# Pooled attention and a rotated channel mixer on one core: another way to load the queries of batch 1, twelve matmuls ahead of the rest, the last stores split over two queues, and a new order of pieces

## The chip, the core and the metric

One NeuronCore of a Trainium2 chip runs the whole kernel. The metric is the device time of one execution in microseconds, as the median of repeated executions. Engines in what follows: PE multiplies matrices and turns tiles (its weight loads are listed as PEld), DVE, ACT and POOL work on elements, SP only issues DMAs.

## What is computed

The attention has 8 batches of 8 heads with 576 positions of 64 channels; its keys and values are first averaged over groups of 8 positions, so that each query meets 72 keys. Its output, put side by side into 512 channels, goes through a layer that rotates by learned angles, mixes over positions and channels, and adds a gated copy.

```python
k_p = k.reshape(B, H, S // 8, 8, D).mean(axis=3); v_p = v.reshape(B, H, S // 8, 8, D).mean(axis=3)
attn = softmax(q @ k_p.T / sqrt(D)); x = (attn @ v_p) put to [B, S, H * D]
theta = x @ w_theta
y = w_tok_r @ (x * cos(theta)) + w_tok_i @ (x * sin(theta))      # over positions
u = x + y
out = u + maximum(u @ w_ch, 0)
```

All four weight matrices arrive as 64-bit floats and are read as pairs of 32-bit words; everything else is 32-bit.

## The kernel before

The work is cut into pieces, each a Python generator whose steps issue a few instructions. For batch b there are: `k`/`K` and `v`/`V` (load keys and values by parts, and add up groups of 8; for batch 0 PE adds them with an identity, L509, for the others POOL or DVE, L435 and L440), `Q` (load queries and turn them so that channels lie on partitions), `S` (scores of 128 positions on PE, L662, the maximum on DVE, L693, the exponential on ACT, L702 or L713, then the division, L727 and L734), `E` or the last steps of `S` (turn the probabilities), `X` (probabilities times values, L856, which gives x by channels in the tile xT), `T` (angles on PE, L879, sine and cosine on ACT, x turned back on PE, L889, and the products z on DVE, L906 and L908), `Z` (split z into a rounded part zh and a rest zl, L930), `M` (the mix over positions, L944, and u = x + y, L950), and `F` (the channel product, L973, the gate, L979, a 32x32 turn, L992, and four stores by SP, L998). A product of two 32-bit matrices is made of three products of rounded parts.

Before the first mix the weights have to be made: `h` (w_theta), `w` (the two position matrices, part 0 and 1 of five row blocks), `W` (their turning on PE, L389 and L392, and the split into WTh on ACT or DVE and WTl on DVE, L400) and `c` (w_ch). The 64-bit floats are put together in `to_f32` (L284 to L317): a scaling on ACT (L292), the low word (L296 on ACT, L298 on DVE or POOL), a sign (L303 on ACT, L305 on DVE or POOL), two integer steps on DVE (L307, L309) and a product (L316 on DVE or POOL).

What order things have is written out by hand in a table, `SCHEDULE` (L30): each word names a piece and issues its next step, and a letter at its end (v, g, a) sets which of DVE, POOL and ACT does the step where there is a choice. Every engine, and SP's queue of DMAs, runs its own instructions in the order of the table and stops at the first one whose input or buffer is not ready.

For batch 0 the queries are loaded by rows, 128 positions of all heads at a time, and turned on PE (`queries_on_pe`, L550, five pieces, with a copy from PSUM by ACT or DVE, L572). For all other batches they are loaded in 16 DMAs of 72 KB, already cut into 32x32 blocks, and DVE turns the blocks (`queries`, L535, two pieces, L547).

```python
EARLY, EXACT, V_ON_PE, K_ON_PE, Q_ON_PE, SUMS_ON_ACT = 2, 1, 1, 1, 1, 2   # L136
for word in SCHEDULE.split():                                              # L1079
    name, engine = (word[:-1], word[-1]) if word[-1] in "vga" else (word, None)
    now[0] = engine
    next(streams[name])
```

## Time and profile before

| what | us |
| --- | --- |
| executions of the kernel: median of 3 (lowest, highest) | 629.72 (628.58, 631.18) |
| the profiled execution, own time | 627.23 |
| its span on the core | 625.5 |
| scores of batch 0's first tile start on PE | 20.23 |
| first mix product (L944) starts on PE | 84.36 |
| first channel product (L973) starts on PE | 121.29 |
| last matmul ends | 619.87 |

The span runs from the first to the last instruction of the profiled execution, which is one of many and here 0.4% under the median of the others. Busy time counts from the start of an instruction to its end, so an instruction that has begun and is held up inside still counts as busy. A stretch of the span tells more than the whole, since the opening (weights and batch 0), the middle and the end have different limits.

### The profile page before, as it was taken

The page shows a single profiled execution, that of the slowest core. Times are in us where ns is not written, and L with a number is a line of the kernel's source. Part 1 is how long each engine was busy: PE and PEld are TensorE (multiplying, and loading weights), DVE is VectorE, ACT ScalarE, POOL GpSimd, SP SyncE. Part 2 cuts the span into 40 slices and gives each one's busy share as a digit, 9 for nine tenths or more (in the row PEclk, how much of TensorE's full clock was granted, in tenths as well). Part 3 has the DMA queues.
Part 4 walks back from the last instruction along what each step waited for, and adds up shares of the span by engine and source line. Part 5 has one row for each costly group of instructions (what it writes and reads, how often), then busy time and mean ns, then how long its engine had stood idle before and what let it go on. Part 6 is the DMA issues. An engine that isn't in the chain of part 4 may idle for free.

```text
span 625.5 us, 11352 instructions
## 1 busy us (share of the span) xinstructions
PE 586.4 (94%) x4076; PEld 541.6 (87%) x4076; DVE 490.0 (78%) x898; ACT 306.4 (49%) x658; POOL 338.4 (54%) x371
## 2 busy tenths in 40 slices
PE   4899889999789999999999999999999989999996
PEld 3765789978689989998999999988999989989996
DVE  5679988888898889898868687798967798856324
ACT  4798858678822564228622762236335443044010
POOL 4566445766766677466463668547445652622230
PEclk9999989999999999999999999999999999999998
DMA  9896202376454555655357346663433231311204
GB/s 281 197 259 156 73 35 77 81 138 119 97 108 68 110 104 109 121 101 94 63 109 120 63 88 112 112 101 57 77 52 74 43 57 24 60 20 27 33 1 76
DMA packets 239912, 57.84 MB, mean 92 GB/s; under 512 B 227952, under 2 KB 228464, under 8 KB 239856
## 3 DMA queue, kind: packets, MB, share of 16 engines
q1 hardware_dynamic: 239856, 57.12, 46.7%
q8 instruction: 32, 0.52, 0.4%
q14 instruction: 24, 0.20, 0.1%
HBM read 37.81 MB, written 9.44 MB: 76 GB/s over the span
## 4 chain that ended last, share of the span: by engine, by line
PE 64%; DVE 17%; ACT 5%; issue 3%; DMA 2%; POOL 2%; SPq 1%; DVEq 0%; POOLq 0%; ACTq 0%
PE py L944 29%; PE pf L973 13%; PE pt L879 11%; PE pv L856 4%; PE s L662 3%; PE px L889 2%; DMA kpst<-in_k_dram 1%; DVE ul L957 1%; DVE mx L693 1%; DVE en L727 1%; DVE e L709 1%; ACT e L702 1%; DVE sm L715 1%; DVE g L885 1%; POOL kpst L435 1%
## 5 line engine op out<-in xcount | busy, mean ns | idle before, releaser
L944 PE MATMUL py<-WTh,zh 128*128 128x256 f32 (+1 forms) x576 | 87.2, 299 | 2.3 <-ACT zh L175 2.3
L944 PE MATMUL py<-WTl,zh 128*128 128x256 f32 (+1 forms) x576 | 87.3, 296 | 0.0
L944 PE MATMUL py<-WTh,zl 128*128 128x256 f32 (+1 forms) x576 | 85.3, 294 | 0.8 <-DVE xT L950 0.5
L944 PEld LDWEIGHTS py<-WTh,zh 128*128 128x128 f32 x576 | 80.8, 191 | 2.7 <-ACT zh L175 2.6
L944 PEld LDWEIGHTS py<-WTl,zh 128*128 128x128 f32 x576 | 80.4, 190 | 0.0
L944 PEld LDWEIGHTS py<-WTh,zl 128*128 128x128 f32 x576 | 77.7, 188 | 1.6 <-DVE xT L950 0.7
L872 POOL TENSOR_TENSOR xl<-xT,xh 128x512 fp32r<-128x512 f32 x31 | 43.3, 1401 | 35.8 <-DVE xh L177 19.4
L950 DVE TENSOR_TENSOR xT<-py,xT 128x256 f32<-128x256 f32 (+1 forms) x64 | 28.2, 445 | 35.9 <-PE py L944 35.4
L930 POOL TENSOR_TENSOR zl<-z,zh 128x1152 fp32r<-128x1152 f32 x14 | 39.1, 2794 | 23.2 <-ACT zh L175 19.0
L957 POOL TENSOR_TENSOR ul<-xT,uh 128x320 fp32r<-128x320 f32 (+1 forms) x36 | 34.9, 975 | 26.6 <-ACT uh L175 17.0
L973 PE MATMUL pf<-uh,chh 128*128 128x320 f32 (+1 forms) x256 | 47.1, 306 | 0.0
L879 PE MATMUL pt<-th,xh 128*128 128x512 f32 x160 | 45.3, 405 | 1.3 <-DVE g L885 1.2
L879 PE MATMUL pt<-th,xl 128*128 128x512 f32 x160 | 43.7, 395 | 1.7 <-DVE xl L872 1.6
L973 PE MATMUL pf<-ul,chh 128*128 128x320 f32 (+1 forms) x256 | 44.5, 296 | 0.0
L973 PE MATMUL pf<-uh,chl 128*128 128x320 f32 (+1 forms) x256 | 44.5, 296 | 0.0
L883 ACT ACTIVATE g<-pt,c_magic 128x512 f32<-128x512 f32 x38 | 26.1, 687 | 36.6 <-PE pt L879 34.1
L879 PE MATMUL pt<-tl,xh 128*128 128x512 f32 x160 | 43.1, 391 | 0.0
L175 ACT CAST uh<-xT 128x256 fp32r<-128x256 f32 (+1 forms) x28 | 11.6, 426 | 64.2 <-DVE xT L950 64.1
L713 ACT ACTIVATE e<-e 128x576 f32<-128x576 f32 (+1 forms) x30 | 20.6, 686 | 45.3 <-DVE e L709 45.1
L885 DVE SCALAR_TENSOR_TENSOR g<-g,pt 128x512 f32<-128x512 f32 x38 | 25.9, 681 | 16.6 <-ACT g L883 16.4
L973 PEld LDWEIGHTS pf<-uh,chh 128*128 128x128 f32 x256 | 37.4, 189 | 1.2
L662 PE MATMUL s<-kpT,qT 128*128 128x144 f32 x256 | 37.6, 289 | 0.9 <-ACT qT L175 0.7
(247 smaller groups left out, 1449.4 us busy)
## 6 DMA issues: line engine op xcount, KB each, us to landing
qsst<-in_q_dram SPq DMA_DIRECT2D x112, 72.0 KB, 2.9
out_dram<-R SPq DMA_DIRECT2D x112, 72.0 KB, 2.1
kpst<-in_k_dram SPq DMA_DIRECT2D x15, 512.0 KB, 5.4
vpst<-in_v_dram SPq DMA_DIRECT2D x28, 256.0 KB, 4.1
eraw<-G SPq DMA_DIRECT2D x96, 60.0 KB, 2.2
eraw<-G SPq DMA_DIRECT2D x96, 40.0 KB, 2.1
WTh_st<-in_moe_w_theta_dram SPq DMA_DIRECT2D x4, 512.0 KB, 4.9
wcraw<-in_moe_w_ch_dram SPq DMA_DIRECT2D x4, 512.0 KB, 3.3
```

Of the source, the lines that this page charges most:

```text
L662: nc.tensor.matmul(scs[c // 2][:n, 2 * SP * (c % 2) : 2 * SP * (c % 2 + 1)], qT[:, c, t0 : t0 + n], kpT[:, c, :], start=True, stop=True,)
L713: nc.scalar.activation(e[:n], e[:n], AF.Exp, scale=scale)
L856: nc.tensor.matmul(pv[:, :gn], l, r, start=i == 0, stop=i == len(terms) - 1)
L872: ENG[pick()].tensor_tensor(xl, xT[:, :, o], f32(xh), ALU.subtract)
L879: nc.tensor.matmul(pt, l[:, c, :], r[:, c, :], start=i == 0, stop=i == 11)
L883: nc.scalar.activation(g, pt, AF.Identity, bias=c_magic)
L885: nc.vector.scalar_tensor_tensor(g, g, MAGIC, pt, ALU.subtract, ALU.subtract)
L930: ENG[pick()].tensor_tensor(zl, z[:, :, o], f32(zh), ALU.subtract)
L944: nc.tensor.matmul(py[:, :n], l[:, kk, :], r[:, kk, t], start=i == 0, stop=i == 3 * NK - 1)
L950: nc.vector.tensor_tensor(u, py[:, :n], u, ALU.add)
L957: ENG[pick()].tensor_tensor(ul[:, c, t], u, f32(uh[:, c, t]), ALU.subtract)
L973: nc.tensor.matmul(pv[:, :n], l[:, kk, o], uhl[r][:, kk, t], start=i == 0, stop=i == 11)
```

## The change

Batch 1's queries are now loaded by rows and turned on PE as batch 0's are: five pieces `Q1.0` to `Q1.4` instead of two, 5 DMAs instead of 16, 20 transposes on PE into the banks "av" and "th", three of the five copies on ACT and two on DVE. A new piece `D` issues twelve products of the identity with itself on PE; it is the first word of the table. Of the last four stores, the second and fourth are issued by ACT, the others by SP. The table is written anew: about the same steps stand before each of the landmarks (first mix, first channel product, each later batch), but in the opening the order of loads and of steps differs, and many steps have another engine letter.

```diff
-EARLY, EXACT, V_ON_PE, K_ON_PE, Q_ON_PE, SUMS_ON_ACT = 2, 1, 1, 1, 1, 2
+EARLY, EXACT, V_ON_PE, K_ON_PE, Q_ON_PE, SUMS_ON_ACT = 2, 1, 1, 1, 2, 2
...
+    def warm_up():
+        p = bank([P, 512], "av", "warm")
+        for _ in range(12):
+            nc.tensor.matmul(p[:, 0:P], ident, ident, start=True, stop=True)
+        yield
...
-        if m < 2:
-            if ("q", b) not in stages:
-                stages["q", b] = staged(b, "qs", 0, 2 * S, "qs")
-            st = stages["q", b][:, DM * m : DM * m + DM]
-        elif m < 4:
-            st = staged(b, "qs", 1, 2 * S, "qs")[:, DM * (m - 2) : DM * (m - 2) + DM]
+        if m < 4:
+            if ("q", b, m // 2) not in stages:
+                stages["q", b, m // 2] = staged(b, "qs", m // 2, 2 * S, "qs")
+            st = stages["q", b, m // 2][:, DM * (m % 2) : DM * (m % 2) + DM]
+        elif b:
+            st = work([64, DM], F32, "kvr", f"qst{b}")
         else:
             st = work([P, DM], F32, "xh", f"qst{b}", bufs=2)
...
-        pq = bank([P, NC, P], "tp" if m % 2 else "px", f"pq{b}_{m}")
+        pq = bank([P, NC, P], (("px", "tp"), ("av", "th"))[b][m % 2], f"pq{b}_{m}")
...
-            nc.sync.dma_start(
+            (nc.scalar if b == B - 1 and c == NC - 1 and i % 2 else nc.sync).dma_start(
...
+    stream("D", warm_up())
...
-w0.0 w0.0 w0.0v h0 h0 k0.0 K0.0 h0g w0.0g w0.0 h2 h1 h0a h0 h0 h1 h0v h0 k0.2 K0.2 h2 h2v h2v h2 h2 h0a h0 h2v
+D k0.2 w0.0 w0.0 w0.0a w0.0v w0.0 h0 h0 h0a k0.0 K0.0 h0a h0 h0 h0v h0 h0v h0 h2 h2 k0.1 K0.1 h2a h2a h1 h2 h2
```

Lines of the new kernel stand 7 lower than before from L259 to L1039. The table's effect is shown at three places.

**The first loads and the first matmuls.** SP's first issues before (kpst, early and kprst hold batch 0's keys, WTh_st a block of w_theta, wraw one of w_tok_r, qsst queries):

```order
L372 DMA wraw_0_106<-in_moe_w_tok_r_dram 128x1152
L321 DMA WTh_st<-in_moe_w_theta_dram 128x1024
L453 DMA kpst_0_116<-in_k_dram 128x2x512
L321 DMA WTh_st<-in_moe_w_theta_dram 128x1024 x2
L465 DMA kprst_140<-in_k_dram 64x512
L563 DMA qsst_0_161<-in_q_dram 128x8x64
L453 DMA early<-in_k_dram 128x2x512
```

and now:

```order
L472 DMA kprst_119<-in_k_dram 64x512
L379 DMA wraw_0_121<-in_moe_w_tok_r_dram 128x1152
L328 DMA WTh_st<-in_moe_w_theta_dram 128x1024
L460 DMA kpst_0_134<-in_k_dram 128x2x512
L328 DMA WTh_st<-in_moe_w_theta_dram 128x1024
L460 DMA early<-in_k_dram 128x2x512
L328 DMA WTh_st<-in_moe_w_theta_dram 128x1024
L570 DMA qsst_0_196<-in_q_dram 128x8x64
```

The second half of the keys (early) moves from seventh to sixth place, and past 768 KB: a block of w_theta and 256 KB of queries come after it, the 128 KB of kprst before everything. PE's first rows before (kpp is the sum of keys, ths w_theta's sum, pq the turned queries, pk and pkr the turned keys, s the scores):

```order
L509 MATMUL kpp_118<-kpst_0_116,ident 128x128 x8
L343 MATMUL ths_137<-WTh_st,ident 128x512
L344 MATMUL ths_137<-WTl_st,identr 128x512
L511 MATMUL kpp_118<-kprst_140,ident 64x64 x8
L570 MATMUL pq_0_163<-ident,qsst_0_161 128x128 x4
L509 MATMUL kpp_118<-early,ident 128x128 x8
L520 MATMUL pk_182<-ident,kp_169 64x128 x4
L530 MATMUL pkr_193<-ident,kpr_170 64x64
L662 MATMUL s_0_200<-kpT,qT_160 128x144 x4
```

and now:

```order
L256 MATMUL warm<-ident 128x128 x12
L516 MATMUL kpp_136<-kpst_0_134,ident 128x128 x8
L350 MATMUL ths_149<-WTh_st,ident 128x512
L351 MATMUL ths_149<-WTl_st,identr 128x512
L516 MATMUL kpp_136<-early,ident 128x128 x8
L518 MATMUL kpp_136<-kprst_119,ident 64x64 x8
L527 MATMUL pk_187<-ident,kp_182 64x128 x4
L577 MATMUL pq_0_198<-ident,qsst_0_196 128x128 x4
L537 MATMUL pkr_206<-ident,kpr_183 64x64
L669 MATMUL s_0_209<-kpT,qT_195 128x144 x4
```

The twelve products stand first; the three parts of the keys' sum are now one after the other, with no turn of queries among them.

**ACT in the opening**, from its first scaling on, before:

```order
L292 ACTIVATE wsrc_a<-wraw_0_106 128x576
L292 ACTIVATE WTh_st<-WTh_st 128x512
L303 ACTIVATE chh_st<-WTh_st 128x512
L292 ACTIVATE WTh_st<-WTh_st 128x512 x2
L347 ACTIVATE th<-ths_137 128x512
L175 COPY qT_160<-pq_0_163 128x4x128
L175 COPY kp_169<-kpp_118 128x128 x2
L175 COPY kpr_170<-kpp_118 64x64
L296 ACTIVATE WTl_st<-WTh_st 128x512
L292 ACTIVATE wsrc_a<-wraw_0_196 128x576
L296 ACTIVATE wsrc_b<-wraw_0_196 128x576
L303 ACTIVATE chh_st<-wsrc_a 128x576
```

and now:

```order
L299 ACTIVATE wsrc_a<-wraw_0_121 128x576
L303 ACTIVATE wsrc_b<-wraw_0_121 128x576
L299 ACTIVATE WTh_st<-WTh_st 128x512
L303 ACTIVATE WTl_st<-WTh_st 128x512
L310 ACTIVATE chh_st<-WTh_st 128x512
L299 ACTIVATE WTh_st<-WTh_st 128x512
L303 ACTIVATE WTl_st<-WTh_st 128x512
L310 ACTIVATE chh_st<-WTh_st 128x512
L299 ACTIVATE WTh_st<-WTh_st 128x512
L303 ACTIVATE WTl_st<-WTh_st 128x512
L175 COPY kp_182<-kpp_136 128x128 x2
L175 COPY kpT<-pk_187 64x4x72
```

The copies of turned keys (kpT) came on DVE before and are ACT's now; the copies of turned queries (qT) and of th were ACT's and are DVE's now; the low words (WTl_st, wsrc_b) and signs (chh_st) of the first blocks, which POOL and DVE made, are ACT's now, and the third block of w_theta stands ahead of the keys' copies.

**Batch 1's queries in SP's queue**, before:

```order
L542 DMA qsst_0_434<-in_q_dram 32x18x32 x8
L372 DMA wraw_0_443<-in_moe_w_tok_r_dram 128x1152
L465 DMA kprst_468<-in_k_dram 64x512
L374 DMA wraw_1_536<-in_moe_w_tok_i_dram 128x128
L375 DMA wraw_1_536<-in_moe_w_tok_i_dram 128x1024
L374 DMA wraw_1_560<-in_moe_w_tok_i_dram 128x128
L375 DMA wraw_1_560<-in_moe_w_tok_i_dram 128x1024
L456 DMA vpst_0_568<-in_v_dram 64x2x512 x2
L372 DMA chh_st<-in_moe_w_tok_r_dram 128x1152
L542 DMA qsst_1_651<-in_q_dram 32x18x32 x8
```

and now:

```order
L381 DMA wraw_1_564<-in_moe_w_tok_i_dram 128x128
L382 DMA wraw_1_564<-in_moe_w_tok_i_dram 128x1024
L472 DMA kprst_568<-in_k_dram 64x512
L570 DMA qsst_0_574<-in_q_dram 128x8x64 x2
L379 DMA chh_st<-in_moe_w_tok_r_dram 128x1152
L463 DMA vpst_0_621<-in_v_dram 64x2x512 x2
L570 DMA qsst_1_672<-in_q_dram 128x8x64 x2
L463 DMA vpst_1_740<-in_v_dram 64x2x512 x2
L328 DMA wcraw_779<-in_moe_w_ch_dram 128x1024
L376 DMA wraw_0_800<-in_moe_w_tok_r_dram 64x1152
L377 DMA wraw_0_800<-in_moe_w_tok_i_dram 64x1152
L570 DMA qst_876<-in_q_dram 64x8x64
```

Sixteen issues of 32x18x32 blocks have become five of whole rows; the first two stand behind the third position block's second part (wraw_1) and the rest of batch 1's keys (kprst), the next behind batch 1's values (vpst).

## Rows read from the trace of the kernel before

**Rows 1.** The page of the whole kernel: busy time of each engine, its share of the span, and its instructions.

```profile
PE 586.4 (94%) x4076; PEld 541.6 (87%) x4076; DVE 490.0 (78%) x898; ACT 306.4 (49%) x658; POOL 338.4 (54%) x371
```

**Rows 2.** Busy time by stage (the windows view): for each stretch its length, then busy us and instructions of PE, PEld, DVE, ACT and POOL, the granted share of TensorE's clock, the DMA share and GB/s.

```profile
0.00:20.00 20.00, 9.55 (x59) 7.48 (x59) 11.69 (x24) 8.73 (x16) 10.31 (x15) 1.00 1.01 275
20.00:49.00 29.00, 25.79 (x181) 19.32 (x181) 20.77 (x43) 25.24 (x112) 17.05 (x22) 1.00 0.89 225
49.00:84.60 35.60, 30.11 (x166) 22.98 (x165) 34.72 (x50) 30.28 (x50) 18.90 (x17) 0.97 0.36 86
84.60:121.50 36.90, 35.66 (x270) 35.41 (x270) 30.75 (x66) 24.29 (x86) 20.04 (x19) 0.98 0.30 73
121.50:200.00 78.50, 70.19 (x496) 64.11 (x495) 68.52 (x125) 48.39 (x109) 52.36 (x63) 1.00 0.56 106
200.00:600.00 400.00, 395.27 (x2763) 372.59 (x2762) 312.88 (x573) 168.34 (x284) 217.54 (x237) 1.00 0.43 76
```

**Rows 3.** Who PE waited for (the waits view of PE: in total, times, longest), first from 40 to 90 us, then from 120 to 200 us.

```profile
PE wt L389 <- DVE WTl L400: 3.4, 3, 1.9
PE pkr L530 <- ACT kpT L175: 2.1, 1, 2.1
...
PE pv L856 <- DVE xT L177: 2.5, 1, 2.5
```

**Rows 4.** PE in the opening (timeline: start us, length us, line, operation, tiles, count, and in brackets the idle time before it and what ended it).

```profile
7.54 3.59 PE L509 MATMUL kpp<-kpst,ident 128*128 128x128 f32 x16 [7.54 <-DMA kpst<-in_k_dram]
12.00 1.13 PE L343 MATMUL ths<-WTh_st,ident 128*128 128x512 f32 x2 [0.86 <-DVE WTh_st L307]
16.18 2.05 PE L509 MATMUL kpp<-early,ident 128*128 128x128 f32 x16 [0.84 <-ACT kp L175]
...
18.07 0.93 PE L520 MATMUL pk<-ident,kp 128*64 128x128 f32 x4
20.23 1.25 PE L662 MATMUL s<-kpT,qT 128*128 128x144 f32 x8
```

**Rows 5.** ACT in the opening (the same view).

```profile
10.44 0.78 ACT L303 ACTIVATE chh_st<-WTh_st 128x512 f16<-128x512 f32 x1 [3.70 <-DVE wsrc_a L307]
...
22.44 0.21 ACT L698 ACTIVATE mx<-mx 128x8 f32<-128x8 f32 x1
...
26.36 0.21 ACT L698 ACTIVATE mx<-mx 128x8 f32<-128x8 f32 x1 [0.82 <-DVE mx L693]
...
35.30 0.30 ACT L719 ACTIVATE sm<-sm,c_eps 128x8 f32<-128x8 f32 x1
```

**Rows 6.** POOL and then DVE in the opening (the same view).

```profile
7.74 1.81 POOL L305 TENSOR_SCALAR chh_st<-wsrc_a 128x576 f16<-128x576 f32 x1
...
9.59 0.76 DVE L307 SCALAR_TENSOR_TENSOR wsrc_a<-wsrc_a,chh_st 128x576 int32<-128x576 int32 x1 [3.46 <-POOL chh_st L305]
11.25 0.69 DVE L307 SCALAR_TENSOR_TENSOR WTh_st<-WTh_st,chh_st 128x512 int32<-128x512 int32 x1 [0.91 <-ACT chh_st L303]
...
19.04 0.91 DVE L177 COPY kpT<-pk 64x288 f32<-64x288 f32 x3 [1.83 <-PE pk L520]
...
29.73 0.69 DVE L727 TENSOR_TENSOR spare<-spare,ri 128x512 f32<-128x512 f32 x1
...
42.49 0.69 DVE L349 TENSOR_SCALAR th<-ths 128x512 fp32r<-128x512 f32 x1
...
47.82 1.23 DVE L400 TENSOR_TENSOR WTl<-wt,WTh 128x1024 fp32r<-128x1024 f32 x1
```

**Rows 7.** SP's queue in the opening (timeline of the issues), and one line of the DMA view from 4 to 15 us (tiles, count, KB each, us from issue to landing) with the bytes moved in that stretch above it.

```profile
4.64 2.38 SPq L453 DMA_DIRECT2D early<-in_k_dram  x1
...
29.94 7.15 SPq L542 DMA_DIRECT2D qsst<-in_q_dram  x8
...
DMA packets 2709, 3.53 MB, mean 321 GB/s; under 512 B 1668, under 2 KB 1668, under 8 KB 2709
...
early<-in_k_dram SPq DMA_DIRECT2D x1, 512.0 KB, 9.3
```

**Rows 8.** The tile qT up to 120 us: instructions that write it, with min/median/max ns and first and last start.

```profile
L177 DVE COPY qT<-pq x3: 416/680/691, 24.3 to 26.2; 128x512 f32<-128x512 f32 x2, 128x256 f32<-128x256 f32 x1
L175 ACT COPY qT<-pq x2: 585/585/585, 15.4 to 22.0; 128x512 f32<-128x512 f32 x2
L547 DVE STREAM_TRANSPOSE qT<-qsst x2: 1365/1367/1369, 49.0 to 63.1; 128x1152 f32<-128x1152 f32 x2
```

**Rows 9.** Busy time around the stop of PE at 80 us (windows view, columns as in Rows 2).

```profile
80.00:82.60 2.60, 0.26 (x2) 0.11 (x1) 2.40 (x4) 2.23 (x7) 2.06 (x2) 0.98 0.00 0
82.60:86.00 3.40, 3.36 (x18) 3.36 (x19) 3.31 (x5) 1.52 (x2) 1.55 (x1) 0.51 0.11 28
```

**Rows 10.** DVE and POOL at 178 us (timeline).

```profile
178.42 3.20 DVE L727 TENSOR_TENSOR en<-e,ri 128x512 f32<-128x512 f32 x1
...
178.29 2.78 POOL L930 TENSOR_TENSOR zl<-z,zh 128x1152 fp32r<-128x1152 f32 x1 [3.05 <-ACT zh L175]
```

**Rows 11.** The end of the kernel: DVE's last instruction and SP's last four issues (timeline), then one line of the windows view (columns as in Rows 2).

```profile
620.37 0.45 DVE L992 STREAM_TRANSPOSE rz<-oT 128x256 f32<-128x256 f32 x1
...
620.84 1.98 SPq L998 DMA_DIRECT2D out_dram<-rz  x4
...
621.70:623.90 2.20, 0.00 (x0) 0.00 (x0) 0.00 (x0) 0.00 (x0) 0.00 (x0) 0.53 0.83 132
```

More of the change, by code (lines that the diff above doesn't have):

```diff
@@ new lines @@
+F1.3.1 F1.2.1 T2.4 Z2.0a F1.3.1 S3.2 F1.3.0 F1.3.0 X3.0.0 X3.0.0v Z2.0v K4 S3.3 S3.3 S3.3v S3.3g M2.0.0 M2.0.0
+X3.0.1 X3.0.1v Z2.1g Z2.1g M2.0.1 S3.4 S3.4 X3.0.2 v4.1 V4.1g M2.0.1 X3.0.2v S3.3 M2.0.0v K4a K4 Z2.3a K4v
+M2.1.0 M2.1.0 k5.2 K5.2g S3.4 S3.4g S3.4g S3.4 X3.0.3 X3.0.3v T3.0a T3.1v F1.2.1 Z2.3v M2.1.1 M2.1.1 Q4.1 k5.0
+K5.0g Z2.2g M2.1.1a M2.1.1v M2.3.0 Z2.2g M2.3.0 M2.3.0g S4.0 S4.0 S4.0 S4.0 S4.0v M2.3.1 M2.3.1 S4.0g T3.0v
+F1.3.1 F1.3.0 E3.2 E3.2g E3.2a M2.1.0a E3.2v M2.1.0g E3.2g M2.3.1a S4.1 M2.3.1g S4.1 S4.0 S4.1 S4.1 M2.2.0 T3.0
@@ new lines @@
+T3.0 M2.2.0 M2.2.0a M2.2.0v S4.1v S4.1g S4.1 M2.2.1 M2.2.1 T3.0 X3.2.0 M2.0.1g X3.2.0a M2.0.0g S4.2 S4.2 M2.0.1g
+M2.3.0g F2.0.0 F2.0.0 Q5.0 S4.2 M2.2.1g M2.2.1v T3.0 k5.1 K5.1g T3.1g S4.2 S4.2g S4.2g F1.3.1 X3.2.1 X3.2.1a
+F2.0.0 F2.0.1 F2.0.1 F2.0.1 X3.2.2 X3.2.2v v5.0 K5 S4.3 S4.3 T3.0 T3.0a T3.0 X3.2.3 X3.2.3a X3.2.3g V4v T3.0
+T3.0 S4.3 S4.3 T3.1 T3.1 F2.0.1 V4g V4 V4g S4.4 T3.1 T3.1 T3.1 Q5.0 F2.1.1 F2.1.1 E4.0 F2.1.0 F2.1.0 F2.1.0
+F2.1.1 F2.1.1 T3.1a T3.1 T3.1 T3.1 T3.2g T3.2g T3.2 T3.2 F2.2.0 T3.2 T3.2 T3.2 V5.0g F2.2.0 T3.2a T3.2 T3.3g
@@ new lines @@
+S7.2g S7.2v F5.3.0 F5.3.0 F5.3.0 F5.3.1 Z6.1g S7.3 S7.3 S7.3 M6.0.0 M6.0.0 X7.0.0 S7.2 S7.3v M6.0.1 M6.0.1
+M6.0.0g M6.0.1v X7.0.0a X7.0.2 X7.0.2a S7.3g S7.3 S7.4 S7.4 S7.4 S7.4 S7.4v S7.4g S7.4 M6.0.1g X7.0.1 M6.1.1
+M6.1.1 X7.0.1a M6.1.1v X7.0.3 X7.0.3a M6.1.0 M6.1.0 Z6.2a M6.1.0v Z6.2g T7.0a T7.0v M6.2.0 M6.2.0 M6.2.0v
+M6.2.0g M6.2.1 M6.2.1 E7.2 E7.2a E7.2v E7.2v E7.2v Z6.3g M6.1.0v Z6.3g M6.3.0 M6.3.0 M6.0.0g T7.1a T7.1g M6.3.1
+M6.3.1 M6.2.1a M6.3.1g M6.3.1v T7.0 T7.0 T7.0 T7.0 T7.0 X7.2.1 X7.2.1v T7.0v T7.0 T7.0 T7.0 M6.1.1g M6.2.1g
@@ new lines @@
+F6.0.1 F6.0.1 X7.2.0 T7.1 X7.2.0a T7.1 T7.1 T7.1 F5.3.1 X7.2.2 X7.2.2a M6.3.0g M6.3.0g F6.0.0 F6.0.0 F6.0.0
+F6.0.1 X7.2.3 X7.2.3a T7.2a T7.2g F6.0.1 F6.1.1 F6.1.1 T7.1 T7.1v T7.1 T7.1 T7.1 T7.2 T7.2 T7.2 F6.1.0 F6.1.0
+F6.1.0 F6.1.1 F6.1.1 T7.2 T7.2 T7.2a T7.2 T7.2 T7.2 X7.2.3v T7.3g T7.3g T7.4a T7.4g T7.3 T7.3 T7.3 T7.3 T7.3
+T7.3v T7.3 T7.3 T7.3 F6.2.0 F6.2.0 T7.4 T7.4 T7.4 T7.4 T7.4 T7.4 T7.4 Z7.0a F6.2.1 F6.2.1 F6.2.0 F6.2.1 F6.2.1
+F6.3.1 F6.3.1 Z7.1v F6.3.0 F6.3.0 Z7.0g M7.0.0 M7.0.0 M7.0.0v F6.3.1 F6.3.0 F6.3.1 M7.0.1 M7.0.1 Z7.1g M7.1.0
```

178 lines of the change are left out of this document (79 added, 99 removed).

## The prediction

> **What bounds the kernel now.** I read the engines' busy times first. PE is busy 586.4 us of the 625.5 us span [rows 1]: whatever the change does, it can win no more than the 39 us in which PE stands, or what PE loses inside its busy time. The windows say where those are [rows 2]. From 200 to 600 us PE works 395.3 of 400 us: nothing to win there, and a DVE or POOL that gets faster changes nothing. From 121.5 to 200 us it stands 8.3 us, from 84.6 to 121.5 us 1.2 us, from 49 to 84.6 us 5.5 us, before 49 us 13.7 us, and after its last matmul there are 5.6 us of stores. So the kernel has a long part in which PE is the limit, and an opening in which it is not.
>
> In the opening the limit changes hands. Up to 20.2 us the keys have to arrive, be added and turned before the first scores can start [rows 4]. From 22.4 to 35.5 us ACT makes four tiles of exponentials almost without a pause [rows 5]. From 49 to 84.6 us DVE is busy 34.7 of 35.6 us while PE and ACT each have over 5 us free [rows 2], and PE's waits in that part name the split of the weights on DVE [rows 3]. Whatever moves the first mix (84.4 us) moves the end, as everything behind it is nearly full PE work.
>
> **The change part by part.** The sum is made against the profiled execution's own 627.23 us; it lies 2.5 us under the median 629.72 of the runs, so I apply the difference to the median.
>
> *Up to the first scores.* SP's new first issues put 128 KB of keys ahead of everything, and take 768 KB from in front of the second half of the keys. The DMAs move 321 GB/s there and this transfer landed at 4.64 + 9.3 = 13.9 us [rows 7]; 786 kB less is 2.4 us, so 11.5 us. The first half landed at 7.54 us [rows 4] and comes 0.4 us later. PE's first sum of keys took 3.59 us for 16 matmuls, the same sum at 16.18 us 2.05 us [rows 4]: at 0.22 and 0.13 us a pass I read the first as run at the lower of the two levels (1.2 of 2.4 GHz). The twelve products (two passes each as these have, so 24 between 0.13 and 0.22 us: 3 to 5.4 us, from about 1.3 us on) end before the keys arrive and cost nothing; what they give is at most those 1.5 us. Next on PE is w_theta's sum. It stood at 12.00 us, waiting for DVE's step at 11.25 us, which waited for ACT's sign at 10.44 us, which waited for DVE's 9.59 us step, which waited 3.5 us for POOL's sign of 1.81 us [rows 4 to 6]. The new table gives that sign to DVE and w_theta's low word and sign to ACT, and the chain starts from ACT alone; I put w_theta's sum at 9.9 to 11.5 us. The second half of the keys then adds from 11.5 to 13.5 us, the rest to 14.6 us. ACT's copies of the sums now stand behind the third block of w_theta, which now has 256 KB less before its end than the keys had, so lands at about 13.1 us, and takes two scalings; the copies end at about 14.9 us. From the turn of the keys to the first scores it was 20.23 - 18.07 = 2.2 us [rows 4]; so the scores start at 17.1 instead of 20.2 us. **Term: -3.1.** Bounds: 0 if the transfers do not come earlier, -4.5 if the third block is not late.
>
> *The four tiles of exponentials.* From 22.44 to 35.5 us ACT loses about 0.9 us, of it 0.82 at 26.36 us where the maximum came late [rows 5]; behind that stood PE's and ACT's handling of queries, which ACT copied and DVE copies now (0.58 us each, 0.68 on DVE, [rows 8]). **Term: -0.8**, bounds 0 and -0.9.
>
> *From there to the first mix.* By the two orders, each instruction priced at the median of its own line and tile, DVE has 32.6 us of work up to the first split of weights (47.8 to 49.0 us, [rows 6]), and 35.3 now: two th (0.69 each), two qT, two signs, two products and two small copies more, the four kpT (0.9 for three) and an en (0.69) less [rows 6, 8]. It was busy 11.7 + 20.8 of these 49 us [rows 2], so 2.7 us fit into the 16.5 free ones. Between that split and the last one DVE has 33.4 us before and 33.6 now: the two turns of batch 1's queries (2 x 1.37) go, a copy from PSUM (0.68), two casts of weights and a sign come. PE gets 20 transposes for batch 1's queries, about 2.2 us, into its 5.5 us of free time, ACT three copies (1.8 us) into 5.3. **Term: 0**; the lead of 3.9 us is carried. If the cover is gone, that is if DVE cannot use its early free time, up to 2.9 us of the lead go.
>
> *SP's queue.* Sixteen issues of 7.15 and about 4 us, at 0.5 to 0.9 each [rows 7], become five. What stood behind them on SP, the third row block of w_tok_r first, is issued earlier. I count nothing, since PE's waits name no DMA from 40 to 90 us [rows 3]. The new loads stand behind the weights' second parts and the rest of the keys; should one be late, PE stops in its own order at the transposes, with w_theta's and the weights' products queued behind.
>
> *First mix to first channel product.* DVE has 28.4 us of work before and 31.6 now (a cast of z, two signs, half a pooling of values). It was busy 30.8 of 36.9 us [rows 2], but PE's one stop of 1.2 us there stood at the end of a run of DVE steps. **Term: +0.8**, bounds 0 and +3.2.
>
> *121.5 to 200 us.* DVE is busy 68.5 of 78.5 us and PE stands 8.3 us; its longest wait is for a copy of DVE's [rows 2, 3]. DVE's work to batch 1's first channel product is 70.9 before and 71.5 now. **Term: 0**, bounds -4 and +3. Behind 200 us PE is full: 0, bounds -1 and +2.
>
> *The end.* DVE ends at 620.82 us; SP issues the last four stores in 1.98 us, and the packets flow from 621.7 to 623.9 us [rows 11]. By the issues alone two queues would save half, 1.0 us. But the engines were busy 0.83 of those 2.2 us [rows 11], so full use saves 0.17 x 2.2 = 0.4. The Trainium skill ("Trainium Kernel Development and Optimization", Key Constraints) says that DMAs of all queues share the same 16 engines and that a second issuing engine only saves issue time; by that rule too the engines' share, not the issue, sets the gain. **Term: -0.4**, bounds 0 and -1.0.
>
> Sum: -3.1 - 0.8 + 0.8 - 0.4 = -3.5. On the profiled execution 623.7, on the median **626.2 us**. A measurement of this kernel can tell about 0.5% (3.1 us) from no change, so the forecast stands just past the bound.
>
> **The rivals.**
> - *DVE keeps the lead.* The steps given to DVE stand in its order behind inputs that come no earlier, and the 97% busy stretch from 49 to 84.6 us ends where it ended. For it: that stretch; against it: 16.5 us free before. The 3.9 us are gone: 629.72 + 0.8 - 0.4 = 630.1. Chance 0.18.
> - *DVE becomes the limit up to the first channel product (slower).* The added 2.7 + 0.2 us before the first mix and 3.2 us behind it are all paid, and the end comes 6.1 - 0.4 = 5.7 us later: 635.4. It decides at the first split of weights: if that ends later than 49.05 us, this is the case. What could do it is DVE held up beside POOL: the division of 512 elements took 3.20 us at 178.42, with a POOL step of 2.78 running, against 0.69 at 29.73 [rows 6, 10]. The Trainium skill ("SBUF — State Buffer", SBUF: two separate sides) has this as a rule: DVE with two inputs in SBUF and POOL take a shared port in turn, and the second waits out the first's whole instruction. The trace agrees at that place. It bears on a table that hands steps from one to the other, but the new one has less POOL work ahead of the first angles, so I hold it for less likely. Chance 0.14.
> - *The middle gains as well.* The waits of 8.3 us halve, and PE does not stop at 80 us, where it stood some 2.3 us and then ran 3.4 us at a granted clock of 0.51 [rows 9], 1.7 us lost. 629.72 - 3.5 - 4 - 1.7 = 620.5. For it: the new table has less POOL work ahead of the angles; against it: the same row of steps (WTh, kpT, then the turn of the last keys on PE) stands there again. Chance 0.20.
> - *The twelve products do not do what they are for.* PE stands from their end (4.3 to 6.7 us) to the keys at about 7.9 us; at 80 us a stop of that length came right before the lower level [rows 9]. Then the first sum takes 3.59 us again and 1.5 us are lost: 627.7. Chance 0.03.
>
> **How the numbers follow.** The forecast has 0.45, with a range of its own of 623.5 to 629. Over 0.5% faster means under 626.6: all of the third rival and somewhat over half of the forecast, 0.20 + 0.28 = 0.48. Within 0.5% (to 632.9): the rest of the forecast and the first and fourth rivals, 0.17 + 0.18 + 0.03 = 0.38. Slower: 0.14. The range takes the third rival's time at its lower end and leaves most of the second out at the upper: 620.5 to 631.5.
>
> **What would show it.** First scores at about 17 us (before 20.23); the fourth tile of exponentials done by 32 us (35.5); the first split of weights done by 45 to 46 us (49.05) and the first mix at about 80.5 us (84.4); from there to the first channel product 37 to 38 us as before; PE's standing from 121.5 to 200 us still about 8 us; the last packets 0.4 us nearer to the last turn. Wrong if the scores do not start earlier (the transfers or the third block of w_theta), if they do and the first mix does not (DVE), or if PE shows waits at the transposes of batch 1's queries.

## Result, and the profile after the change

The changed kernel takes 634.75 us in the median of its first 7 executions (632.80 to 635.37) against 629.88 of the kernel before on the same chip: ratio 1.0066, 95% interval 1.0045 to 1.0088. It is slower, by 4.2 us by the ratio and 4.9 by the medians, where 3.5 us less were forecast. A second set of 12 executions gives 1.0069 (1.0043 to 1.0094). The profiled execution took 635.37 us, its span is 633.6 us.

The page's first line answers to [rows 1]: PE is busy 16 us longer with 44 matmuls more, DVE 8 us less over the whole kernel, POOL 16 us more.

```profile
PE 602.3 (95%) x4120; PEld 556.4 (88%) x4120; DVE 482.1 (76%) x893; ACT 300.8 (47%) x655; POOL 354.1 (56%) x382
```

The windows by stage answer to [rows 2] (columns as there); the stages now end at the end of the first split of weights, at the first mix and at the first channel product:

```profile
0.00:20.00 20.00, 14.93 (x92) 13.22 (x93) 13.00 (x25) 10.89 (x20) 5.21 (x12) 0.93 0.99 270
20.00:52.40 32.40, 29.42 (x175) 21.88 (x175) 21.72 (x44) 22.33 (x107) 15.51 (x18) 0.83 0.76 207
52.40:88.00 35.60, 32.99 (x184) 25.68 (x184) 32.06 (x53) 29.54 (x49) 19.19 (x20) 0.92 0.33 80
88.00:130.30 42.30, 38.99 (x270) 38.28 (x269) 35.93 (x68) 23.38 (x85) 18.61 (x18) 0.91 0.30 74
...
200.00:600.00 400.00, 394.66 (x2752) 372.55 (x2751) 308.51 (x566) 162.45 (x276) 246.30 (x260) 1.00 0.44 77
```

Three things are to be read here. The first split of weights ends at 52.4 us instead of 49.05, and the first channel product starts at 130.3 instead of 121.29; from there to the end of the last matmul it is 496.5 us, before 498.6. So all of the loss is made before the first channel product: 3.4 of these 9 us stand at the first split, 0.2 more come up to the first mix, and 5.4 between the first mix and the first channel product. Up to it DVE has 102.7 us of work (the four stages added) against 97.9 in [rows 2], POOL 58.5 against 66.3: over the whole kernel DVE got lighter, in the opening it got heavier. And the granted clock, 1.00 nearly everywhere before, is 0.83 to 0.93 in all four stages. The same view cut where the clock changes:

```profile
7.10:17.30 10.20, 7.23 (x59) 5.97 (x59) 6.22 (x12) 5.87 (x12) 0.00 (x0) 1.00 1.15 329
17.30:31.00 13.70, 11.55 (x48) 10.21 (x49) 7.12 (x14) 7.13 (x40) 5.61 (x6) 0.50 1.08 247
31.00:82.20 51.20, 48.15 (x296) 35.58 (x294) 43.56 (x79) 42.64 (x115) 28.03 (x31) 1.00 0.48 130
82.20:92.40 10.20, 9.32 (x48) 8.22 (x47) 6.96 (x12) 4.51 (x10) 5.46 (x4) 0.50 0.19 66
92.40:123.10 30.70, 27.39 (x208) 26.68 (x208) 28.49 (x49) 18.35 (x61) 10.97 (x9) 1.00 0.15 46
123.10:126.50 3.40, 3.40 (x15) 3.40 (x14) 3.22 (x9) 2.73 (x17) 1.35 (x2) 0.50 1.35 226
```

TensorE stood at the lower of its two levels (1.2 of 2.4 GHz) for 27 us behind its first rise, in the kernel before for 3.4 us before the last matmul. (Up to that first rise the column shows 1.00 all the same; there the level is read from the lengths of the products: the twelve took 0.23 us a pass, the sum of keys behind them 0.13.) PE's timeline answers to [rows 4]:

```profile
1.35 5.49 PE L256 MATMUL warm<-ident 128*128 128x128 f32 x24 [1.35 <-POOL ident masks.py:199]
8.80 2.02 PE L516 MATMUL kpp<-kpst,ident 128*128 128x128 f32 x16 [1.96 <-DMA kpst<-in_k_dram]
...
16.38 0.41 PE L527 MATMUL pk<-ident,kp 128*64 128x128 f32 x2 [0.84 <-ACT kp L175]
...
18.10 2.26 PE L669 MATMUL s<-kpT,qT 128*128 128x144 f32 x8
...
26.87 2.26 PE L669 MATMUL s<-kpT,qT 128*128 128x144 f32 x8 [0.87 <-DVE ri L731]
```

The twelve products run as planned, the first sum of keys takes 2.02 us instead of 3.59, and the first scores start 2.1 us earlier. But a tile's scores now take 2.26 us, not 1.25. The lead is gone by the third tile of exponentials, where ACT waits for a maximum, and at the first split the kernel is 3.4 us late (first ACT, then DVE):

```profile
30.91 0.21 ACT L705 ACTIVATE mx<-mx 128x8 f32<-128x8 f32 x1 [3.32 <-DVE mx L700]
```

```profile
51.18 1.23 DVE L407 TENSOR_TENSOR WTl<-wt,WTh 128x1024 fp32r<-128x1024 f32 x1
```

### The profile page after: what moved, and what is told of

Its sections match the earlier page's. It is cut to its first block, busy times and chain, and to the rows that moved or that the text cites. A ratio compares the mean times of both kernels' runs of the same rounds, so it can differ in the third digit from the quotient of the medians.

```text
span 633.6 us, 11412 instructions
## 1 busy us (share of the span) xinstructions
PE 602.3 (95%) x4120; PEld 556.4 (88%) x4120; DVE 482.1 (76%) x893; ACT 300.8 (47%) x655; POOL 354.1 (56%) x382
## 4 chain that ended last, share of the span: by engine, by line
PE 66%; DVE 17%; SPq 6%; ACT 3%; DMA 3%; issue 2%; POOL 0%; DVEq 0%; ACTq 0%; POOLq 0%
PE py L951 24%; PE pf L980 13%; PE pt L886 13%; SPq L816 6%; PE pv L863 6%; PE s L669 3%; PE px L896 2%; DMA eraw<-G 2%; DVE ul L964 1%; DVE mx L700 1%; DMA kpst<-in_k_dram 1%; DVE G L750 1%; PE pq L577 1%; PE s L661 1%; DVE en L734 1%
## 5 line engine op out<-in xcount | busy, mean ns | idle before, releaser
L951 PE MATMUL py<-WTl,zh 128*128 128x256 f32 (+1 forms) x576 | 88.8, 300 | 0.0
L951 PEld LDWEIGHTS py<-WTl,zh 128*128 128x128 f32 x576 | 82.0, 194 | 0.0
L937 POOL TENSOR_TENSOR zl<-z,zh 128x1152 fp32r<-128x1152 f32 x20 | 55.1, 2759 | 31.4 <-ACT zh L175 19.1
L879 POOL TENSOR_TENSOR xl<-xT,xh 128x512 fp32r<-128x512 f32 x33 | 44.6, 1357 | 43.6 <-ACT xh L175 30.8
L964 POOL TENSOR_TENSOR ul<-xT,uh 128x256 fp32r<-128x256 f32 (+1 forms) x40 | 33.8, 857 | 34.0 <-ACT uh L175 18.9
L669 PE MATMUL s<-kpT,qT 128*128 128x144 f32 x256 | 40.8, 306 | 2.0 <-DVE ri L731 0.9
L175 ACT COPY xT<-pv 128x320 f32<-128x320 f32 (+1 forms) x43 | 17.1, 398 | 50.2 <-PE pv L863 46.9
L669 PEld LDWEIGHTS s<-kpT,qT 128*128 128x128 f32 x256 | 36.3, 203 | 3.8 <-ACT spare L709 1.2
L980 PEld LDWEIGHTS pf<-ul,chh 128*128 128x128 f32 x256 | 38.0, 189 | 1.7 <-DVE ul L964 1.7
```

The costliest lines, as they stand in the source:

```text
L669: nc.tensor.matmul(scs[c // 2][:n, 2 * SP * (c % 2) : 2 * SP * (c % 2 + 1)], qT[:, c, t0 : t0 + n], kpT[:, c, :], start=True, stop=True,)
L879: ENG[pick()].tensor_tensor(xl, xT[:, :, o], f32(xh), ALU.subtract)
L937: ENG[pick()].tensor_tensor(zl, z[:, :, o], f32(zh), ALU.subtract)
L951: nc.tensor.matmul(py[:, :n], l[:, kk, :], r[:, kk, t], start=i == 0, stop=i == 3 * NK - 1)
L964: ENG[pick()].tensor_tensor(ul[:, c, t], u, f32(uh[:, c, t]), ALU.subtract)
L980: nc.tensor.matmul(pv[:, :n], l[:, kk, o], uhl[r][:, kk, t], start=i == 0, stop=i == 11)
```

## Experiments

Two theories stood against each other at first: the low clock makes the loss, brought by the twelve products or by stops of the new order; or DVE does, which has more to do in the opening (the slower rival of the forecast). Every result has a ratio to the kernel before on the same chip, with its 95% interval.

**The same kernel again, and each small part by itself.**

a1, no edit. 

> The changed kernel once more, not a letter altered, for a second trace of it. Theory (the granted clock falls more often in the changed kernel because PE's activity in the opening is thin at some places): its trace shows the low level again before 130 us, some 15 to 30 us of it in sum, though where it begins may shift, and 632 to 636 us. Rival (the three low stretches of the first trace were an accident of that execution and the lost time is waits): at most 5 us of low clock, and still 632 to 636.

Measured 636.54 us, 1.0069 (1.0043 to 1.0094). Its trace has the low level again, at 8.9 to 12.3, 19.1 to 32.8, 84.0 to 94.2 and 124.9 to 128.3 us: no accident. The scores start at 20.02 us there. In the traces of a3 and a4 below, which have the same steps up to there, they start at 20.00 and 20.93, so the 2.1 us of the first trace are not there in each execution.

a2, the kernel before with the twelve products only:

```diff
+    stream("D", warm_up())
...
+D w0.0 w0.0 w0.0v h0 h0 k0.0 K0.0 ...
```

> The kernel before with nothing added but the twelve identity products, first on PE. If they do what the forecast had for them (first sum of keys at the high level, nothing else): 628 to 630, that is -1.5 to 0. If raising the clock early is what lets it fall again before 20 us (the rise of the kernel before came at 10.8 us, behind the thin part): a low stretch between 14 and 31 us appears, and 631 to 634.

Measured 0.9997 (0.9971 to 1.0023). The products do bring a fall, in the windows of its trace (columns as before) not long behind a stop of PE of 2.27 us that ended at 11.87 us. The faster sum of keys only ended earlier and made the wait for w_theta longer (0.86 us before, [rows 4]):

```profile
6.50:13.30 6.80, 3.60 (x21) 2.37 (x20) 2.86 (x5) 1.55 (x3) 2.85 (x2) 1.00 1.14 329
13.30:26.90 13.60, 11.44 (x54) 9.25 (x53) 5.43 (x13) 4.81 (x11) 3.03 (x2) 0.50 0.99 220
```

The second sum of keys falls into it, and takes 3.78 us instead of 2.05. What the first sum gains the second gives back, and in this trace the scores start 3.3 us later (23.54) and the first split 4.8 us later (52.62) than in that of the kernel before. Over all executions the products are worth nothing that can be told.

b1, the changed kernel without them (the word D and its stream taken out). 

> The changed kernel without the twelve products. If they alone bring the low clock of the opening (the kernel before with them alone had 13.7 us of it at 13 us): no low stretch between 14 and 31 us, but the one at 80 to 94 us stays; about 2 to 3 us less than the changed kernel, 632 to 633.5. If the new order of pieces is thin enough by itself: low stretches before 35 us here too, and 634.5 to 637.

Measured 635.71 us, 1.0075 (1.0050 to 1.0101), with low stretches at 20.9 to 24.3, 37.9 to 41.3, 119.8 to 123.3 and 143.7 to 147.1 us. So the loss is not theirs: it stays without them, low stretches in the opening included.

a3, one queue at the end:

```diff
-            (nc.scalar if b == B - 1 and c == NC - 1 and i % 2 else nc.sync).dma_start(
+            nc.sync.dma_start(
```

> The changed kernel with all four last stores on SP again. If the second queue saves what the forecast said (0.4 us): 635. If, as the two traces have it (from the last element step's start to the span's end 6.7 us with two queues, 5.5 with one), the second queue costs: 1.2 us less, 633.5, and 5.5 us of tail.

Measured 634.67 us, 1.0063 (1.0039 to 1.0086): no difference that can be told from a1, and neither of my two tails: its own is 5.4 us and was to be 5.5, but the time did not fall by 1.2. The traces say why nothing was won. In a1 ACT issues its two stores at once, SP its own only 2.0 us after the turn, and the DMA share has a hole (windows of a1, columns as before):

```profile
630.30:631.30 1.00, 0.00 (x0) 0.00 (x0) 0.00 (x0) 0.00 (x0) 0.00 (x0) 1.00 0.78 125
631.30:632.30 1.00, 0.00 (x0) 0.00 (x0) 0.00 (x0) 0.00 (x0) 0.00 (x0) 1.00 0.16 25
632.30:633.30 1.00, 0.00 (x0) 0.00 (x0) 0.00 (x0) 0.00 (x0) 0.00 (x0) 1.00 0.84 134
```

From the end of the last turn to the end of the span it is 5.2 to 5.8 us in all nine traces with two queues, and 4.4 to 4.6 in ten of the eleven with one (4.63 before). The eleventh is a3 itself, 5.4 us, where SP's second pair was also issued only 2.0 us after the turn (0.9 before). What holds SP there was not found.

**Which part of the order.** The tables issue nearly the same steps before each landmark, so a kernel can follow one up to there and the other behind.

a4, the changed order up to the first channel product, then that of before. 

> The changed kernel whose table goes on in the order of before from the first channel product on (same steps, other order behind it). If the loss sits in the opening (clock and waits up to 133 us): 633 to 636, as the changed kernel. If it sits in the new order behind it (the first output comes 4 us late in batch 1 and 7 us late at the end): 630 to 632.5.

c3, the order of before up to the first mix, then the changed one. 

> The kernel before up to the first mix, then the changed order (no twelve products, queries in blocks, stores by SP). If the loss is made before the first mix (clock, first splits): 629.5 to 631.5. If a good part is made between the first mix and the first channel product (42.3 us there in the changed kernel against 36.9, with a stop of 3.1 us of PE behind DVE): 632 to 634, with the stop at the probabilities' turn and a low stretch behind it.

d2, the changed order up to the first turning of weights (about 45 us), then that of before. 

> The kernel before with the changed order of pieces up to the first turning of weights (about 45 us), then the order of before (no twelve products, queries of batch 1 in blocks, stores by SP). If the first 45 us make the loss: 633 to 635.5, the first split of weights at 51 to 54 us. If the turning of the weights makes it: 629.5 to 631.5, the first split at 47 to 49.

d3, the order of before up to 45 us, then the changed one. 

> The other half: the order of before up to the first turning of weights, then the changed order, with batch 1's queries on PE and two queues at the end, without the twelve products. If the first 45 us make the loss: 630.5 to 632.5 (the 1.5 us behind the first mix stay). If the turning of the weights makes it: 633.5 to 636, the first mix at 87 to 90 us with the first split at 47.8.

```diff
-SCHEDULE = words of one table
+SCHEDULE = words of one table up to F0.0.0 (a4), M0.0.0 (c3) or W0 (d2, d3), then the rest in the other's order
```

Measured: a4 1.0081 (1.0050 to 1.0112), c3 1.0020 (0.9998 to 1.0041), d2 1.0062 (1.0033 to 1.0092), d3 1.0023 (1.0001 to 1.0044). The order behind the first channel product is innocent (a4 loses as much as the changed kernel). The first 45 us alone make a loss as large as the whole one (d2), the rest about 1.4 us (c3, d3); the parts need not add up, since each meets another neighbour. For c3 the interval includes no loss at all. d2's split came earlier than the 51 to 54 us that I expected. In d2's trace the scores start at 19.73 and the first split at 49.91 us (20.23 and 47.82 before): half a microsecond ahead, then 2.1 behind. (The stretch between the two, 27.6 us before, is 27.6 in all seven traces with the order of before up to there and no low level in between: before, b6, c3, d1, d3, d4 and e1.) The chain of waits shows what lies between (start, length, what). Before, from 29.6 to 38.3 us, it is ACT:

```profile
29.97 2.33 ACT e L702 x15
...
32.75 2.53 ACT spare L702 x16
...
36.01 0.73 ACT wsrc_a L292
...
37.50 0.74 ACT chl_st L303
```

and in d2 it is DVE at nearly every step from 27.2 to 33.7 us and from 39.4 us on, with PE in between, where a low level falls on it (35.9 to 39.3 us; w_theta's sum takes 2.00 us there, 1.06 in the chain of before):

```profile
29.10 0.99 DVE spare L723
30.09 0.40 DVE spare L730
30.48 0.73 DVE mx L689 x2
31.21 0.38 DVE wpow L305
...
31.62 0.77 DVE wsrc_b L312
...
36.69 2.00 PE ths L339 x2
...
42.51 0.46 DVE chl_st L301
42.97 0.34 DVE eraw L305
43.31 0.61 DVE WTh_st L303
...
44.41 0.57 DVE WTl_st L312
```

The products wsrc_b and WTl_st were POOL's before, the sign chl_st was ACT's.

f1 takes such work off DVE again, in d2:

```diff
-        nc.vector.scalar_tensor_tensor(ti, ti, 3, sign, ALU.logical_shift_left, ALU.bitwise_or)
+        nc.vector.scalar_tensor_tensor(
+            ti[:, :or_], ti[:, :or_], 3, sign[:, :or_], ALU.logical_shift_left, ALU.bitwise_or
+        )
...
+        yield from to_f32(..., *((64, 64) if c == 3 else ()))
```

(and likewise the two steps behind, for three blocks of w_tok). 

> The kernel d2 (changed order up to 45 us, then that of before) with seven integer steps and products on DVE in that part cut from 512 or 576 columns to 64: for the last block of w_theta and for three blocks of w_tok, whose upper columns so stay unfinished numbers. About 3.5 us of DVE's work between 28 and 46 us goes, nothing else. If DVE is the limit there: the first split of weights starts 1.5 to 3.5 us earlier than d2's 49.9, and 632 to 634 against d2's 635.3. If ACT, PE or the loads set it: the split within 0.5 us of 49.9 and 635.

Measured 631.16 us, 1.0015 (0.9986 to 1.0044): 3.0 us under d2 by the ratios, 4.2 by the medians, with 3.0 us less on DVE (the seven steps took 4.5 us in d2's trace and 1.5 here). Its split, in DVE's timeline:

```profile
48.57 1.22 DVE L401 TENSOR_TENSOR WTl<-wt,WTh 128x1024 fp32r<-128x1024 f32 x1
```

That is 1.3 us earlier than d2's although its scores start 1.3 us later (20.99), so the stretch between them is 2.6 us shorter, and as long as in the kernel before. DVE's work in the first 45 us does make a loss: taken off, it gives back most of it. By the intervals the 3.0 us are uncertain by some 2.6 either way. But not all of the 2.6 us of the trace is DVE's own time: in d2's trace the clock was low for 3.4 us of this stretch, which by the two levels can be worth up to half of that (1.7 us, an estimate), and in f1's trace it did not fall before 76 us. The mean granted clock over all executions rises too, from 0.984 to 0.989.

How much is the clock's and how much DVE's can be read from traces of the same stretch. From the first scores to the first split (windows, columns as before; first before, then the changed kernel, a4, d2 and f1):

```profile
20.23:47.82 27.59, 24.88 (x178) 18.84 (x178) 19.59 (x42) 23.85 (x109) 15.99 (x20) 1.00 0.89 221
18.10:51.18 33.08, 30.10 (x176) 23.33 (x177) 21.76 (x45) 22.41 (x106) 15.96 (x18) 0.81 0.81 212
20.93:49.42 28.49, 24.92 (x176) 18.67 (x177) 21.89 (x46) 22.15 (x106) 16.97 (x18) 1.00 0.82 227
19.73:49.91 30.18, 26.42 (x177) 19.46 (x178) 23.80 (x47) 21.66 (x105) 17.13 (x18) 0.94 0.77 188
20.99:48.57 27.58, 24.51 (x176) 18.57 (x177) 20.30 (x47) 21.47 (x105) 17.14 (x20) 1.00 0.74 193
```

Up to the first channel product a4 runs the very steps of the changed kernel. In its trace the clock was low from 8.1 to 14.9 us and then not before 79.8, and this stretch took 28.5 us. In the changed kernel's two traces and in a3's, 12.7 to 12.9 us of the stretch were at the low level, and it took 33.0 to 33.1. So at the high clock the changed order is 0.9 us longer than that of before there, with 2.3 us more of DVE's work, and the low level adds some 4.6 us. DVE is busy only 21.8 of the 33.1 us: up to 33.7 us the chain of the changed kernel's first trace runs mostly on PE's slow scores and turns. What takes work off DVE helps in two ways, then, directly and through a clock that falls less; that the second follows from PE's shorter waits is likely but not shown by itself.

**Can DVE's load simply be handed back?** c1 and c4 keep the changed order, with the engine letters of before (up to the first mix, or everywhere):

```diff
-... w0.0 h0 h0 h0a k0.0 K0.0 h0a h0 ...
+... w0.0 h0 h0 h0 k0.0 K0.0 h0g h0a ...   (each step the letter that it had before)
```

> The changed kernel's order of pieces with the engine letters of before on every step up to the first mix (39 letters differ; batch 1's queries and the twelve products as changed). Theory (DVE got POOL's work in the opening: 103.1 us busy up to the first channel product against 98.2, POOL 58.8 against 66.8): DVE's busy time up to the first mix falls by 2 to 4 us, the first split of weights starts 1.5 to 3 us earlier for the same clock, and 632 to 634. Rival (the order, not the engine, makes the loss): 635 to 637.

> The changed kernel's order with the engine letters of before on every step to the end (283 letters differ). If the engine choice makes the loss up to the first channel product, also behind the first mix: 631 to 633, and no 3 us stop of PE behind DVE at 120 us. If the letters fit only the order they were chosen for: 636 to 642, with PE waits behind 130 us.

Measured 1.0385 (1.0346 to 1.0424) and 1.1688 (1.1632 to 1.1744). My expectation fell for both; the rival's direction was right, its size far too small. PE's waits in c1 (total, times, longest) have one that neither kernel has:

```profile
PE pe L759 <- POOL spare L731: 6.9, 1, 6.9
```

POOL reaches that division behind a product for which it stood 10.5 us waiting for DVE. The letters belong to their order.

c2, batch 1's queries in blocks again, in the changed order:

```diff
-EARLY, EXACT, V_ON_PE, K_ON_PE, Q_ON_PE, SUMS_ON_ACT = 2, 1, 1, 1, 2, 2
+EARLY, EXACT, V_ON_PE, K_ON_PE, Q_ON_PE, SUMS_ON_ACT = 2, 1, 1, 1, 1, 2
```

> The changed kernel with batch 1's queries loaded as 32x32 blocks and turned on DVE again (16 DMAs and two DVE turns where the new loads and copies stood). If PE's turning of queries is worth what the forecast had for it (0: two DVE turns of 1.37 us against one copy on DVE, three on ACT and 2.2 us of PE): 634.5 to 637. If it frees DVE where DVE is the limit: 1.5 to 3 us more, 637 to 639. If the row loads or the copies hold PE up: 632 to 634.

Measured 1.0201 (1.0172 to 1.0230). Most of it is one stop, and says more of the place I gave the second half than of the queries:

```profile
PE wt L392 <- DVE WTl L403: 9.7, 1, 9.7
```

**The clock by itself.** If PE's stops bring the falls, products in the gaps should hold the clock up. b2 puts them into the changed kernel, b5 and d1 into the kernel before with the twelve, b6 and d4 only into its stop at 80 us:

```diff
+        while True:
+            p = bank([P, 512], "th", "fill")
+            for _ in range(2):
+                nc.tensor.matmul(p[:, 0:P], ident, ident, start=True, stop=True)
+            yield
...
-... K1 K1a K1 K1a ...
+... K1 K1a D D D D K1 K1a ...
```

> The changed kernel with pairs of further identity products where PE stood: 6 behind the twelve, 2 ahead of the turn of the keys, 2 ahead of the turn of their rest, 2 and 4 ahead of the second and third scores, 6 ahead of the fourth row block's turning and 4 at the turn of batch 1's keys. If the low clock is the cause: no low stretch between 7 and 90 us, and about 14 to 20 us of it less at 0.33 us each (the slope over all runs so far), that is 4.5 to 6.5 us under the changed kernel: 629 to 631. If the waits of the new order are the cause: clock up, time within 1.5 us of the changed kernel, 634 to 636.

> The kernel before with the twelve products and further identity products in PE's gaps: 2 behind the twelve, 8 ahead of w_theta's sum, 2 ahead of the second sum of keys, 4 ahead of the turn of the keys' rest, 2 ahead of the second scores, and 8 at the turn of batch 1's keys at 80 us. If the low clock is what the twelve products bring: no low stretch from 7 to 120 us, and 626.5 to 628.5 (12 us of low clock per run in the kernel before, half of it behind the last matmul, at 0.33, and 1 us from the keys' first sum). If the clock is of no weight in the opening of that order: 629.5 to 631.

> The kernel before with eight identity products at the turn of batch 1's keys alone (PE stood 2.06 us there, and the 3.4 us behind ran at a granted clock of 0.51). If that stop brings the fall: no low stretch at 80 us and 1 to 1.7 us less, 628.5 to 629.3. If products in a gap hold PE up, or the fall comes from elsewhere: 630 to 631, the stretch still there.

> The kernel before with the twelve products and single products in PE's gaps, fewer than in b5: 5 ahead of w_theta's sum, 1 ahead of the second sum of keys, 2 ahead of the turn of the keys' rest, 5 at the turn of batch 1's keys (at 0.36 us each, as eight took 2.92 us, so 1.8 us into gaps of 2.3 and 2.1). If the twelve are worth 1.3 us at equal clock and the low clock costs 0.30 us per us: low time 8 to 12 us, and 628 to 629.5 against 630.6 for before. If products in the gaps cost more than the clock they hold up, as in b5: 631 to 633.

> The kernel before with five identity products, not eight, at the turn of batch 1's keys alone (1.8 us into the 2.06 us stop). If the fall behind that stop is what it costs: low time 8 to 9 us instead of 12 and 1.0 to 1.7 us less than before, 629 to 629.6. If the products do nothing: 630.6.

Measured: b2 1.0061 (1.0038 to 1.0083), b5 1.0038 (1.0017 to 1.0060), b6 0.9982 (0.9963 to 1.0001), d1 1.0026 (0.9999 to 1.0054), d4 0.9998 (0.9972 to 1.0023). Of the fill at 80 us alone nothing that can be told came: in b6's and d4's traces the clock stayed high there but fell at 50.3 and 74.9 us instead, and the 1 to 1.7 us that I expected did not show beyond the noise. b5's trace has one short low stretch, at 76.0 to 79.4 us, and the kernel is still 2.4 us slower. Eight products took 2.92 us where PE had stood 2.06 in the kernel before, so they hold up what stands behind them on PE; that this makes all of the 2.4 us is not shown. In b2's trace the clock is high until 34.3 us, over the scores of the first four tiles, and the first split started at 49.12 us, 2.1 us earlier than in the changed kernel's trace; the time did not follow, and my expectation of 629 to 631 fell. Since the products cost time of their own, b2 can't say what the clock alone is worth; a4 shows it, for one stretch. It does not pay to buy the clock with products in PE's own queue.

What goes with a low clock over a whole execution can be read from the executions themselves, since each has its own mean granted clock. Over 308 executions in 20 series, each series with a level of its own, one microsecond more at the low level (twice the missing share of the clock times the span) goes with 0.31 us more (standard error 0.02). The kernel before has 12 us of it on average, of which some 4 lie behind the last matmul, the changed one 24 over its two sets, so some 4 us, most of its loss, go with the clock. Of d2's 3.9 us it is 2.7 (20 us at the low level, 11 in the kernel before on that chip), of f1's 0.9 us it is 0.8. This is not a cause beside the order: b1 and d2 have the falls without the twelve products, and f1, with less work on DVE, has fewer. How much DVE costs without the clock is known only for that stretch, 0.9 us. The Trainium skill ("TensorE: Matmul & The Clock Gate", Terms) prices throttled time at the share of the clock that is held back, which is half of it at this level; the 0.31 measured here is under that. One reason can be that PE is not the limit in the opening all the time.

**A version that beats both.** d3's trace reaches the first mix at 82.4 us, 2 us before the kernel before, although its order behind loses them (the first channel product comes at 123.8 us there). e1 takes only this part of the change: the new order from the first turning of weights to the first mix, with batch 1's queries by rows on PE, and everything else as before.

```diff
-SCHEDULE = words of before
+SCHEDULE = words of before up to W0, then the changed ones up to M0.0.0, then the rest of before
```

> The order of before, with the changed order only from the first turning of weights (45 us) to the first mix, batch 1's queries by rows on PE; no twelve products, last stores by SP. If the 2 us that d3's trace gains up to the first mix reach the end: first mix at 82 to 83 us, first channel product 37 us later, and 628 to 629.5 against 630.7 for before. If DVE or PE gives them back up to the first channel product: 630 to 631.5.

Measured 627.23 us, 0.9955 (0.9929 to 0.9982): 2.8 us faster. Its windows from 49 us on (columns as before):

```profile
49.00:82.50 33.50, 30.88 (x184) 24.19 (x183) 30.68 (x51) 29.54 (x50) 18.41 (x19) 1.00 0.30 76
82.50:119.50 37.00, 34.53 (x265) 34.09 (x263) 31.50 (x68) 24.50 (x87) 19.27 (x18) 1.00 0.26 67
```

DVE is busy 30.7 us up to the first mix instead of 34.7 [rows 2]: the two turns of 1.37 us are off it [rows 8], which is 2.7 of the 4 us, and the 20 transposes fit into PE's free time. The clock does not fall before 183 us. Over its 12 executions the low level lasts 8 us on average against 11 before, so by the slope above 1.1 of the 2.8 us go with the clock. What the loads by rows and what the order in this part win was not taken apart.

## Why the prediction was wrong

The step that failed is the one between the exponentials and the first mix, "Term: 0; the lead of 3.9 us is carried". The slower rival stood beside it, with the test that decides: a first split that ends later than 49.05 us. It ended at 52.4. Its time, 635.4, is 0.65 us from the measured one; I gave it 0.14. That the figure is so near is in part luck: that rival paid only for added DVE work, held up beside POOL, while most of the measured loss goes with a clock that falls more often (some 24 us at the low level against 12). For that my sum had no term behind the first scores; I had put it at nothing without a reason.

- *Up to the first scores, -3.1.* Measured -2.1, -0.2, -0.2 and +0.7 in four traces of the same steps (the changed kernel, a1, a3, a4). The first half of the keys was added from 8.80 us, 1.3 us later than before, not 0.4. w_theta's sum (10.66 us) and the second sum of keys (11.76) came where I had put them, in the first trace. The copies of the sums did not end at 14.9 but at 16.3 us: ACT's second waited for DVE's small one at 15.82, behind four steps for w_theta. That copy was in my count of DVE's work, not in my chain.
- *The twelve products.* The first sum of keys gained 1.6 us, as said. My fourth rival asked whether the clock falls again before the keys; it fell behind them, for 13.7 us, and a2 shows that this eats the gain.
- *Four tiles of exponentials, -0.8.* From the first maximum on ACT to the end of the fourth tile it is 15.8 us, not 13.1 less 0.8: the scores ran at the low level (2.26 us a tile instead of 1.25) and DVE's maxima came late.
- *From there to the first mix, 0.* I set 2.7 us more DVE work against 16.5 free us of 49 and found it covered. The amount was right (34.7 us up to the split, 35.3 forecast), the place was not: half of these 16.5 us lie before 20 us, the rest behind waits, and in d2's trace the chain runs on DVE for most of its steps from 27 us on. From the first scores to the split the new order takes 0.9 us more at the high clock (a4) and 5.5 us more with the low stretch that it had in three of its traces. A stage's free time is not free time at the place where the work falls.
- *First mix to first channel product, +0.8.* Measured +5.4 in the changed kernel (42.3 against 36.9 us), +3.4 in c3 and +4.5 in d3, over the bound of +3.2 that I had kept for "all of it is paid". This step failed as well. Its parts are DVE's longer chain, shown below, and low stretches of the clock (7.9 us in the first trace, 4.8 in c3's, 3.4 in d3's).
- *121.5 us on, 0.* Right in sum: from the first channel product to the end of the last matmul it takes 496 to 500 us in both kernels and in c3, d2, d3, e1 and f1.
- *SP's queue, 0.* PE's waits name no load from 40 to 145 us: right.
- *The end, -0.4.* Measured +0.6 to +1.2 in the traces, and +0.4 by the ratios of a1 and a3, which can't be told from none. The DMA share was not the limit: SP's pair was late.
- *What I did not see.* In the turning of the weights I weighed PE's 20 transposes and DVE's two turns as equal. With the order of this part they were worth 1.8 us up to the first mix (e1); which of the two wins them is not shown.

Between the first mix and the first channel product, where the chain of the changed kernel runs on DVE for most of its steps from 94 to 123 us, its neighbour matters: a step that takes 0.69 us alone [rows 6] took 3.06 beside a POOL step that had begun 0.25 us earlier. In the timelines of POOL and DVE of the changed kernel:

```profile
103.14 2.77 POOL L937 TENSOR_TENSOR zl<-z,zh 128x1152 fp32r<-128x1152 f32 x1 [11.45 <-PE py L951]
```

```profile
103.39 3.06 DVE L314 SCALAR_TENSOR_TENSOR wcts<-wcts,wpow 128x512 int32<-128x512 int32 x1
```

The DVE step ends 0.54 us after POOL's, as the rule quoted with that rival has it (the Trainium skill, "SBUF — State Buffer", SBUF: two separate sides). PE then stood for the probabilities that DVE divides (its waits from 92 to 145 us):

```profile
PE pe L762 <- DVE en L734: 2.6, 2, 2.3
PE per L770 <- DVE er L784: 1.2, 2, 0.8
```
